# Three edits at the handover of a hashed-attention and feed-forward kernel: an earlier split, a later threshold, outputs added by transfer

## The chip, the cores and the metric

The kernel runs on one core of one Trainium2 chip. The metric is the device time of one execution in microseconds; the time before is the median of three runs, 980.2 us (979.35 to 982.82).

## What is computed

The first part is attention with a hash mask, for 4 batches of 8 heads, 768 rows and 64 columns a head; the second is a feed-forward network over the 3072 tokens of all batches, 512 to 2048 to 512.

```python
q_bits = (einsum('bhsd,dk->bhsk', q, proj) > 0)        # 6 bits a row; k likewise
mask = q_bucket[:, :, :, None] == k_bucket[:, :, None, :]
scores = np.where(mask, (1 / sqrt(64)) * q @ k.T, -1e9)
attn = softmax(scores)                                 # over the keys
x = (attn @ v).transpose(0, 2, 1, 3).reshape(3072, 512)
h = x @ w_in
g = h * np.clip(h + 3.0, 0.0, 6.0) / 6.0
out = g @ w_out
```

## The kernel before, in words

**Units of work.** There are 32 heads (i = 8 b + h) and 6 row tiles of 128 rows in each, so 192 row tiles, numbered g or k. Every fp32 operand is held as a rounded high part and a low part, and a product is the sum of two or three products of parts. The scores of a row tile are four matrix products on TensorE (lines 376 and 378); `lowest` (line 385, VectorE) takes the row minimum of the negated scores, `exponential` (397, ScalarE) the softmax numerator. P is then transposed, and `split_p` casts it into the high part ph (464, ScalarE) and subtracts for the low part pl (468, VectorE, or 466, GpSimd). Two row tiles make one output unit u (three in a head; unit numbers run from 0 to 95 over all heads): `values` or `values_whole` (489, 501) multiplies P by v into a bank acc of PSUM.

**Output of a unit.** `output` (lines 513 to 540) copies acc to the tile y (531, ScalarE). Half the rows of acc hold the product with v's high part, the other half that with its low part, and both have to be added. For most heads this is done in memory: one half is stored by a plain transfer from SyncE's queue (537) into xs, and the other half waits in the list `adds`, until `add` (508 to 511) sends it as an adding transfer from GpSimd's queue. For the last head of a batch (`last_head`, 526) ScalarE copies only one half (528), VectorE adds the other (529), and one plain store brings the sum.

**The order of the steps.** The engines' programs are in the order in which the Python code calls them for TensorE, VectorE, ScalarE and GpSimd, transfers issued from GpSimd among them; the order on SyncE's queue, from which all other transfers go, is left to the scheduler. The main loop runs over k. In step k it transposes tile k, takes the exponential of k + 1 and the minimum of k + 2, multiplies by v for an earlier unit, calls `lead(k + 3)` and splits tile k. `lead(j)`, with t = j mod 6, issues the scores of tile j and, depending on t, the preparation of the next heads: at t = 1 and 4 `add`, at t = 3 the hash products (`hash_qk`, 330 to 332) and their thresholding (`bits`, 341, VectorE, with a transfer of the result), at t = 4 `scale_q` (276, GpSimd).

Batch 0's feed-forward part runs as a block of its own, from 142 to 300 us. From k = 94 (`held`) the generator `ffn` is called in the loop and prepares the first chunk of 256 tokens of batch 1: it loads it (xr), inverts the softmax sums, spreads each inverse over 64 columns (`spread`, 559, GpSimd, one buffer), transposes that on TensorE (`rt`, 569, in one of the four banks that pt and acc also use) and multiplies (572, VectorE). Each piece is put beside a step: spread and rt pair of one quarter of the chunk follow each other through steps 95 to 99. From k = 101 (GT - 1) `beside_ffn` takes over: P is transposed by VectorE (`flip`, 418), written to memory (fd) and read back in the order wanted (`move`), and one sixteenth of a chunk's products goes beside each step (`gemm1`, 642; `gate`, 664, 665, 670, 671; `gemm2`, 680 to 685). The buffer p of a tile has two copies, so the minimum of tile 104 needs tile 102 to be written out. The first chunk's split into xh (631, ScalarE) and xl (632, VectorE) stands in the list `opening`, and line 1114 calls it in step 102, ahead of that step's first `gemm1`. A later chunk is begun when its units are out and no add of its batch is pending (`there`, 908).

Of the kernel before, what the change touches and what calls it, by code (L numbers as in the profile page):

```python
# [18 lines left out]
P = 128  # L19
# [9 lines left out]
LA = 3  # L29
# [14 lines left out]
def lsh_attention_moe(  # L44
# [11 lines left out]
    B, H, D, S = qkT.shape  # L56
    D //= 2
    DM, DF = w_in.shape
    KT = S // P
# [16 lines left out]
    def dma(out: bass.AP, in_: bass.AP):  # L76
        nonlocal last
        last = nc.sync.dma_start(out=out, in_=in_)  # L78
# [152 lines left out]
    GF = 2 * HK + FS  # L231
    GT = GF + FT
# [128 lines left out]
    scs, probs, outs = {}, {}, {}  # L361
# [53 lines left out]
    def flip(g: int):  # L415
        nonlocal written
        x = probs.pop(g)[0][:].rearrange("p c k -> p (c k)")
        nc.vector.transpose(x, x)  # L418
        d = dp.tile([P, S], F32, name=f"fd{g}", tag="fd", bufs=4)
        dma(out=d[:], in_=x)  # L420
        written[g] = d, last
# [84 lines left out]
    adds = []  # L506
# [6 lines left out]
    def output(un: int):  # L513
        nonlocal vdone
        i, u = divmod(un, KT // 2)
        b, h = divmod(i, H)
        o = (h % 2) * D
        acc = accs.pop(un)

        if u != 1:  # L520
            outs[i] = sp.tile([P, 4 * P if u == 0 else 2 * P], F32, name=f"y{i}_{u}", tag=f"y{u}", bufs=1)
        y = outs[i][:, 2 * P :] if u == 1 else outs[i][:, : 2 * P]

        r = slice(o, o + D)
        r2 = slice(D - o, 2 * D - o)
        last_head = h == H - 1 and (b > 0 or u == 2)
        if last_head:
            nc.scalar.copy(y[r], acc[r2])
            nc.vector.tensor_add(y[r], acc[r], y[r])
        else:  # L530
            nc.scalar.copy(y, acc[:])
        if u or last_head:
            c = slice(2 * u * P, 2 * (u + 1) * P) if last_head and b else slice(0, 4 * P) if u == 1 else slice(4 * P, S)
            to = xs[b][h * D : (h + 1) * D, c]

            with tc.issue_after(copied.ins):
                dma(out=to, in_=y[r] if last_head else outs[i][r])
            if not last_head:
                adds.append((i, to, outs[i][r2]))
        vdone = 2 * un + 2  # L540


# [33 lines left out]
    muls = []  # L576
# [132 lines left out]
    side, opening = [], []  # L709
# [366 lines left out]
    with tc.manual_schedule(engines={ET.PE, ET.DVE, ET.Activation, ET.Pool}):  # L1076
        split_qk(0, None)
        hash_qk(0)
        bits(0)
        scale_q(1)  # L1080
        split_v(0)
        for x in range(3):
            ahead(0, x)
        for _ in range(2):
            cv(0)
        def go(part: str):
            if stage == part:
                next(fill, None)

        through = []  # L1090

        def beside_ffn(k: int):

            nonlocal paced, stage, held
            held = False
            if k < GT:
                for c in range(2):
                    transp(k, c)  # L1100
                exponential(k + 1)
            for _ in range(2):
                u = vnext // 2
                if u < NS // 2 and (2 * u < GT or k % 2 and k >= 2 * u + 3):
                    if vnext % 2 == 0 and k >= GT:
                        value_whole()
                        through.append(u)
                        break
                    if value_half():
                        through.append(vnext // 2 - 1)  # L1110
                if k < GT:
                    break
            if k == GT:
                opening.pop()()
            if k + 2 < NS and k >= GT:
                lowest(k + 2)
            go("A")
            if k < GT:
                for c in range(2):
                    split_p(k, c, False)  # L1120
                split_lows()
                while through:
                    output(through.pop(0))
                flip(k + 1)
            if k + 2 < NS:
                if k < GT:
                    lowest(k + 2)
                exponential(k + 2)
            paced = True
            multiply()  # L1130
            if k + 2 < NS:
                flip(k + 2)
            if GT <= k - LT < NS:
                for c in range(2):
                    split_p(k - LT, c, False)
            split_lows()
            go("B")
            if k == NS + LT:
                homes.clear()
            while through and (through[0] < vnext // 2 - 1 or k % 2 == 0 or k < GT):  # L1140
                output(through.pop(0))
            hashed = k + LA < NS and (k + LA) % KT == 4 and (k + LA) // KT + 1 < NJ
            if hashed:
                hash_qk((k + LA) // KT + 1)
            go("C")
            if hashed:
                bits((k + LA) // KT + 1)
            if k + LA < NS:
                lead(k + LA)
            if moves:  # L1150
                moves.pop(0)()
            if GT <= k + 1 < NS:
                move(k + 1)

            place_in_chunk = (k - GT) % NFC
            if subs and (k % 2 and (k < GT or place_in_chunk != NFC - 1) or k > GT and place_in_chunk == 0):
                subs.pop(0)()
            go("D")
            if k % KT in (1, 3):
                add()  # L1160

        for k in range(NS + LT + 2):
            if k >= GT - 1:
                beside_ffn(k)
                continue
            end = GB if k < GB else NS
            i, t = divmod(k, KT)
            if k == HK - XE:
                lent += lents[cc3:]
            if k == GB:  # L1170
                lent.clear()
            if k == HK:
                late["x"] = sp.tile([P, S], F32, name="late", tag="raw", bufs=1)
            for c in range(2):
                transp(k, c)
            if k + 1 < end:
                exponential(k + 1)
            if k + 2 < end:
                lowest(k + 2)
            if k == GB:  # L1180
                next(first)
                pair_turn = 0

            third = True
            whole = False
            for _ in range(1 if k != HK else 2):
                if vnext < k - k % 2:
                    whole = value_half()
            held = k >= GF - 2
            if held:  # L1190
                next(fill, None)
            if whole and k >= GF:
                output(vnext // 2 - 1)
                whole = False

            hashed = k >= GF and (k + LA) % KT == 2
            if k >= GF and k + LA < end and not hashed:
                lead(k + LA)
            for c in range(2):
                split_p(k, c, third)  # L1200
            split_lows()
            multiply()
            held = False
            if (k < GF or hashed) and k + LA < end:
                if hashed:
                    if (k + LA) // KT + 1 < NJ:
                        hash_qk((k + LA) // KT + 1)
                        bits((k + LA) // KT + 1)
                    next(fill, None)
                lead(k + LA)  # L1210
            if k == GB - 2:
                hash_qk((GB - 1) // KT + 1)
                bits((GB - 1) // KT + 1)
            if whole:
                output(vnext // 2 - 1)
            if k >= GF - 2 and not hashed:
                next(fill, None)
            if k < GB:
                for f in early_steps[k]:
                    f()  # L1220

            if k < HK and t == 1 and i:
                with tc.issue_after(last.ins):
                    load_w(i)
            if k == HK:
                add()
                late_x()
                with tc.issue_after(last.ins):
                    get_qk(H + 2)
                    for n in range(WE, WL):  # L1230
                        load_w(n)
            if k + 1 == GB:
                first = first_ffn(lambda part: ahead(GB, part))
                next(first)
                for _ in range(2):
                    whole = value_half()
                output(vnext // 2 - 1)
                next(first)
        paced = False
        assert vnext == NS and not through  # L1240
        add()
        for _ in fill:
            pass
# [47 lines left out]
```

## Time and profile before

| what | value |
| --- | --- |
| median of three runs | 980.2 us |
| the profiled execution | 981.36 us |
| its span | 979.6 us |
| TensorE (PE) busy, granted clock | 953.1 us (97%), 0.998 |
| VectorE (DVE) busy | 715.7 us (73%) |
| ScalarE (ACT) busy | 626.7 us (64%) |
| GpSimd (POOL) busy | 479.2 us (49%) |
| adding transfers from GpSimd (line 510) | 57, 48.7 us |
| sums on VectorE (line 529) | 10, 4.3 us |
| chain that ended last: PE, DVE, issue | 77%, 9%, 4% |

Busy time is the time in which an engine executes; a row of the timeline gives start, duration, engine, line and operation, the number of instructions merged into it, and in brackets how long the engine was idle before and what ended that. A matrix product's row can overlap the next one, as products are pipelined. PEclk is the granted clock of TensorE as a share of 2.4 GHz.

### The profile page before, as it was taken

To read this page: it belongs to the slowest core of one execution; us is meant where nothing else is said; L and a number is where in the kernel's file an instruction comes from. 1 tells how busy PE (TensorE), PEld (TensorE's weight loads), DVE (VectorE), ACT (ScalarE), POOL (GpSimd) and SP (SyncE) were. 2 spreads that over 40 slices of the span, in tenths; PEclk is the share of its full clock that TensorE was granted. 3 is DMA by queue.
4 is the path that set the end of the run, shared out by engine and by line. 5 is a ranking of instruction groups with operands and counts; after the bars stand their busy time and mean duration, and the time that the engine had idled before them with its cause. 6 is when DMAs were issued, how large, how long until landed. Compare 5 with 4: busy or idle time off the path is not lost.

```text
span 979.6 us, 19386 instructions
## 1 busy us (share of the span) xinstructions
PE 953.1 (97%) x6306; PEld 874.4 (89%) x6306; DVE 715.7 (73%) x1462; ACT 626.7 (64%) x1421; POOL 479.2 (49%) x498
## 2 busy tenths in 40 slices
PE   8999999999999998899999999999999999999997
PEld 7999888999989998799889888998999899899896
DVE  7999988888569998777777777877777874343422
ACT  6898875656478897567766666766766664333332
POOL 6777744656537775355555545546556542000000
PEclk9999999999999999999999999999999999999999
DMA  4566579100035554687797787797797772101000
GB/s 118 138 165 174 132 229 376 46 2 1 6 121 130 117 114 118 184 246 235 217 274 231 230 244 234 225 272 231 233 267 228 220 222 78 43 1 44 1 22 22
DMA packets 113116, 151.65 MB, mean 155 GB/s; under 512 B 13764, under 2 KB 82116, under 8 KB 113016
## 3 DMA queue, kind: packets, MB, share of 16 engines
q1 hardware_dynamic: 108456, 144.79, 48.8%
q0 software_dynamic: 4560, 5.64, 4.6%
q8 instruction: 50, 0.82, 0.4%
q14 instruction: 50, 0.41, 0.1%
HBM read 77.34 MB, written 53.61 MB: 134 GB/s over the span
## 4 chain that ended last, share of the span: by engine, by line
PE 77%; DVE 9%; issue 4%; POOL 3%; DMA 3%; ACT 2%; SPq 1%; DVEq 0%; ACTq 0%; POOLq 0%
PE h L642 25%; PE po L685 6%; PE po L680 6%; PE po L681 6%; PE acc L489 6%; PE acc L501 5%; PE s L376 5%; PE pt L407 5%; PE s L378 5%; DVE p L385 3%; DVE pl L468 2%; POOL pl L466 2%; DVE qq L341 1%; DMA px<-fd 1%; SPq L78 1%
## 5 line engine op out<-in xcount | busy, mean ns | idle before, releaser
L397 ACT ACTIVATE p<-p,m 128x768 f32<-128x768 f32 x192 | 180.2, 938 | 97.0 <-DVE p L385 91.3
L385 DVE TENSOR_SCALAR_CACHE_REDUCE p<-s 128x768 f32<-128x768 f32 x192 | 183.0, 953 | 45.4 <-PE s L378 30.8
L665 DVE SCALAR_TENSOR_TENSOR h<-g,h 128x256 f32<-128x256 f32 x192 | 81.9, 427 | 95.2 <-ACT g L664 93.5
L664 ACT ACTIVATE g<-h,three 128x256 f32<-128x256 f32 x192 | 90.8, 473 | 91.4 <-PE h L642 89.7
L642 PE MATMUL h<-xh,w 128*128 128x256 f32 x1024 | 146.8, 283 | 1.6 <-ACT xh L631 1.6
L642 PEld LDWEIGHTS h<-xh,w 128*128 128x128 f32 x1024 | 135.5, 189 | 5.1 <-ACT xh L631 1.8
L418 DVE STREAM_TRANSPOSE p<-p 128x768 f32<-128x768 f32 x90 | 88.0, 978 | 60.3 <-ACT p L397 60.3
L466 POOL TENSOR_TENSOR pl<-spare,ph 128x384 fp32r<-128x384 f32 x45 | 62.1, 1381 | 119.0 <-ACT ph L464 82.8
L376 PE MATMUL s<-kk,qq 76*128 76x384 f32 x384 | 101.4, 345 | 4.8 <-DVE qq L341 3.0
L468 DVE TENSOR_TENSOR pl<-pt,ph 128x384 fp32r<-128x384 f32 x196 | 100.0, 550 | 3.6 <-ACT ph L464 3.0
L670 ACT CAST gb<-h 128x256 fp32r<-128x256 f32 x141 | 52.4, 372 | 76.1 <-DVE h L665 43.1
L378 PE MATMUL s<-kk,qq 128*128 128x384 f32 x384 | 100.6, 343 | 0.0
L681 PE MATMUL po<-w,gb 128*128 128x512 f32 x250 | 98.4, 394 | 0.0
L680 PE MATMUL po<-w,gb 128*128 128x512 f32 x250 | 98.4, 394 | 0.0
L466 POOL TENSOR_TENSOR pl<-px,ph 128x384 fp32r<-128x384 f32 x45 | 61.3, 1362 | 75.2 <-ACT ph L464 66.0
L464 ACT CAST ph<-pt 128x384 fp32r<-128x384 f32 x196 | 85.9, 472 | 15.1 <-PE pt L407 13.1
L216 POOL TENSOR_TENSOR w<-wr,w 128x128 fp32r<-128x128 f32 x128 | 71.8, 591 | 45.3 <-ACT w L210 42.4
L407 PE MATMUL pt<-ident,p 128*128 128x128 f32 x612 | 86.0, 274 | 3.6 <-DVE pl L468 2.7
L407 PEld LDWEIGHTS pt<-ident,p 128*128 128x128 f32 x612 | 71.7, 141 | 11.2 <-PE pt L407 2.5
L376 PEld LDWEIGHTS s<-kk,qq 76*128 76x128 f32 x384 | 65.7, 190 | 17.9 <-DVE qq L341 8.0
L642 PE MATMUL h<-xl,w 128*128 128x256 f32 x512 | 81.5, 281 | 0.0
L685 PE MATMUL po<-w,gb 128*128 128x512 f32 x250 | 78.7, 395 | 0.0
(153 smaller groups left out, 2130.9 us busy)
## 6 DMA issues: line engine op xcount, KB each, us to landing
fd<-p SPq DMA_DIRECT2D x90, 384.0 KB, 3.0
spare<-fd SPq DMA_DIRECT2D x180, 96.0 KB, 2.6
px<-fd SPq DMA_DIRECT2D x180, 96.0 KB, 3.2
kk<-qq SPq DMA_DIRECT2D x62, 192.0 KB, 3.3
wr<-in_w_in SPq DMA_DIRECT2D x16, 512.0 KB
wr<-in_w_out SPq DMA_DIRECT2D x16, 512.0 KB, 7.5
raw<-in_qkT SPq DMA_DIRECT2D x19, 384.0 KB, 3.8
vr<-in_v SPq DMA_DIRECT2D x32, 192.0 KB, 3.4
```

The costliest lines, as they stand in the source:

```text
L376: nc.tensor.matmul(s[:, c, :HW], lhsT=q1[:KM, us], rhs=half(k1[:KM], c), start=True, stop=False)
L378: nc.tensor.matmul(s[:, c, :HW], lhsT=q2[:, us], rhs=half(k2, c), start=False, stop=True)
L385: nc.vector.tensor_scalar(out=pr_[:], in0=s[:, :, :HW], scalar1=CAP, scalar2=None, op0=ALU.min, op1=ALU.min, accum_out=m[:],)
L397: nc.scalar.activation(pr_[:], pr_[:], AF.Exp, bias=m[:], scale=-1.0, accum_out=sms[b][:, t, h : h + 1])
L407: nc.tensor.transpose(pt[:, x], probs[g][0][:, c, x * P : (x + 1) * P], ident[:])
L466: engine.tensor_sub(lo, pt, hi.bitcast(F32))
L468: lows.append(lambda: engine.tensor_sub(lo, pt, hi.bitcast(F32)))
L642: nc.tensor.matmul(hp, lhsT=wi[:, wp, wc], rhs=x[cc][xp], start=(k == 0 and cc == 0), stop=(k == 2 and cc == NCC - 1),)
L664: nc.scalar.activation(r[:], hp, AF.Relu, bias=three[:], scale=1.0)
L680: nc.tensor.matmul(po[u], lhsT=gh[:, us], rhs=wo[:, 0], start=(fc == 0), stop=False)
L681: nc.tensor.matmul(po[u], lhsT=gh[:, us], rhs=wo[:, 1], start=False, stop=False)
L685: nc.tensor.matmul(po[u], lhsT=gl[:, us], rhs=wo[:, 0], start=False, stop=(fc == NFC - 1))
```

## The change

It does three things. In `output`, for batches 1 to 3, only the first unit (u = 0) of the last head is still added on VectorE; the second and the third are copied in full, one half is stored and the other goes into `adds`. The call of `opening` moves from the beginning of step 102 to step 101, behind `flip(102)` and ahead of `lowest(103)` and `exponential(103)`. In the plain loop from k = 96 on, a step with (k + 3) mod 6 = 3 calls `lead` behind `split_p`, `split_lows` and `multiply`, as one with remainder 2 already did; in that step `lead` holds the hash products, the scores and `bits`.

```diff
-        last_head = h == H - 1 and (b > 0 or u == 2)
+        last_head = h == H - 1 and u == (0 if b else 2)
...
         if u or last_head:
-            c = slice(2 * u * P, 2 * (u + 1) * P) if last_head and b else slice(0, 4 * P) if u == 1 else slice(4 * P, S)
+            alone = last_head or h == H - 1 and b
+            c = slice(2 * u * P, 2 * (u + 1) * P) if alone else slice(0, 4 * P) if u == 1 else slice(4 * P, S)
             to = xs[b][h * D : (h + 1) * D, c]
 
             with tc.issue_after(copied.ins):
-                dma(out=to, in_=y[r] if last_head else outs[i][r])
+                dma(out=to, in_=y[r] if alone else outs[i][r])
             if not last_head:
-                adds.append((i, to, outs[i][r2]))
+                adds.append((i, to, y[r2] if alone else outs[i][r2]))
...
-            if k == GT:
-                opening.pop()()
             if k + 2 < NS and k >= GT:
                 lowest(k + 2)
             go("A")
...
                 flip(k + 1)
+                assert len(side) <= 2 and not muls
+                opening.pop()()
             if k + 2 < NS:
                 if k < GT:
                     lowest(k + 2)
...
             hashed = k >= GF and (k + LA) % KT == 2
-            if k >= GF and k + LA < end and not hashed:
+            after = hashed or k >= GF and (k + LA) % KT == 3
+            if k >= GF and k + LA < end and not after:
                 lead(k + LA)
...
-            if (k < GF or hashed) and k + LA < end:
+            if (k < GF or after) and k + LA < end:
```

## Rows read from the trace of the kernel before

**Rows 1.** Stretches: length, busy time (instructions) of each engine, PEclk, DMA share, GB/s
```profile
380.00:400.00 20.00, 17.40 (x125) 15.59 (x123) 16.12 (x33) 12.27 (x28) 8.75 (x9) 1.00 0.36 101
400.00:410.00 10.00, 7.35 (x38) 6.59 (x37) 6.42 (x15) 5.61 (x15) 0.00 (x0) 0.83 0.80 241
```

**Rows 2.** PE's waits, 380 to 412: total us, times, longest us
```profile
PE h L642 <- ACT xh L631: 1.6, 1, 1.6
PE pt L407 <- DVE pl L468: 1.5, 3, 1.0
PE rt L569 <- DVE y L529: 1.1, 1, 1.1
```

**Rows 3.** Timeline, VectorE and ScalarE, steps 96 to 102
```profile
381.97 0.48 ACT L464 CAST ph<-pt 128x384 fp32r<-128x384 f32 x1 [0.46 <-PE acc L489]
...
383.43 1.09 DVE L341 TENSOR_SCALAR qq<-z,thr,val 44x768 fp32r<-44x768 f32 x1 [0.86 <-issue]
...
384.55 1.02 DVE L468 TENSOR_TENSOR pl<-pt,ph 128x384 fp32r<-128x384 f32 x2
...
386.99 0.37 ACT L528 COPY y<-acc 64x256 f32<-64x256 f32 x1 [3.35 <-PE acc L489]
...
388.14 0.43 DVE L529 TENSOR_TENSOR y<-acc,y 64x256 f32<-64x256 f32 x1
...
401.54 0.98 DVE L418 STREAM_TRANSPOSE p<-p 128x768 f32<-128x768 f32 x1 [1.15 <-ACT p L397]
402.44 1.39 DVE L632 TENSOR_TENSOR xl<-xr,xh 128x256 fp32r<-128x256 f32 x4
```

**Rows 4.** Timeline, TensorE, steps 96 to 102
```profile
383.89 0.39 PE L569 MATMUL rt<-ident,spare 128*128 128x128 f32 x2
385.26 0.98 PE L407 MATMUL pt<-ident,p 128*128 128x128 f32 x6 [0.98 <-DVE pl L468]
...
388.72 0.41 PE L569 MATMUL rt<-ident,spare 128*128 128x128 f32 x2 [1.05 <-DVE y L529]
...
391.21 0.38 PE L569 MATMUL rt<-ident,spare 128*128 128x128 f32 x2
...
394.61 0.52 PE L407 MATMUL pt<-ident,p 128*128 128x128 f32 x3 [0.24 <-DVE pl L468]
...
401.85 2.36 PE L642 MATMUL h<-xh,w 128*128 128x256 f32 x8 [1.60 <-ACT xh L631]
```

**Rows 5.** Groups of instructions: busy us, mean ns, idle before, releaser
```profile
L531 ACT COPY y<-acc 128x256 f32<-128x256 f32 x86 | 31.6, 368 | 6.8 <-PE acc L489 4.8
```

**Rows 6.** Timeline, SyncE's queue and GpSimd, steps 88 to 98
```profile
365.86 0.46 SPq L78 DMA_DIRECT2D xs<-y  x1
...
368.63 0.83 POOL L510 DMA_DIRECT2D xs<-y  x1 [1.57 <-DMA xs<-y]
...
387.98 2.14 POOL L276 TENSOR_SCALAR raw<-raw 64x768 f32<-64x768 f32 x1 [3.18 <-DMA raw<-in_qkT]
390.07 0.39 POOL L559 COPY spare<-rc 128x256 f32<-128x256 f32 x1
```

**Rows 7.** PE's waits, 412 to 820
```profile
PE acc L501 <- POOL pl L466: 1.8, 8, 0.3
```

**Rows 8.** Timeline, GpSimd, first chunk of the last batch
```profile
829.83 0.40 POOL L559 COPY spare<-rc 128x256 f32<-128x256 f32 x1 [2.71 <-PE rt L569]
```

**Rows 9.** Stretches of one microsecond behind the first product, columns as in rows 1
```profile
403.00:404.00 1.00, 1.00 (x5) 1.00 (x6) 0.83 (x3) 0.00 (x0) 0.00 (x0) 0.50 1.06 424
```

**Rows 10.** The chain that ended last, 398 to 413: start us, us, what
```profile
400.75 3.49 DMA fd<-p
404.35 0.98 DVE p L385 x2
...
407.71 0.88 DVE p L385 x2
...
412.66 0.62 PE s L376 x2
```

## The prediction

> **What bounds the kernel now.** I read the page's busy shares first: TensorE (PE) is busy for 97% of the span, the others for 73% at most. So an edit that moves work of other engines pays only where PE stands still. The table of stretches shows where: from 380 to 400 us PE misses 2.6 of 20, and from 400 to 410, where attention hands over to the mixed phase, 2.65 of 10, at a mean granted clock of 0.83 [rows 1]. The three edits act in steps 95 to 102, some 376 to 410 us, and one of them also at the last heads of batches 2 and 3. Next come PE's waits from 380 to 412: 1.6 us for the first token chunk's rounded halves (xh), 1.5 in three for P's low parts, the longest 1.0, and 1.1 for the output add on VectorE (DVE) [rows 2]. These are what the three edits touch. The profiled run took 981.36 us, 1.76 of them outside its span of 979.6; the median of the runs is 980.2, 1.16 lower. I work out differences in the profiled run and put them on the median. About 0.5%, 4.9 us, is what a measurement of this kernel can tell from no change.
>
> **Bits behind the low parts.** The condition holds once in the plain loop: for k from 96 to 100, (k+3) mod 6 is 3 only at k = 96, and the case that was there before, 2, does not come. In that step DVE sits idle for 0.86 us, then runs head 17's bits at 383.43 for 1.09, then both low parts in 1.02; the ph casts that these need end at 382.45 (381.97 + 0.48) [rows 3]. PE has finished the rt transposes at 384.28 and waits until 385.26, 0.98 us, because the next pt tiles take the banks that the low parts free [rows 4]. Swapped, the low parts start at about 382.6 and the banks are free at 383.6, before PE asks. The bits start at 383.6 instead of 383.43, and their transfer goes out 0.2 later; head 17's scores are three steps off, which hides that. The PE order does not change, since the step issues nothing for PE between the two places. The gain is 0.98 here. It could be 0 if DVE's next wait swallowed it, but the value products and the y copy that follow wait for PE alone.
>
> **Last heads' units.** Each of three batches loses two adds on DVE (0.43 each) and gets two adding transfers from GpSimd (POOL). The ScalarE copies stay, 128 rows wide instead of 64: 368 ns on average [rows 5] against the 0.37 us of the one at 386.99 [rows 3], so no cost. What goes: rt at 388.72 waits 1.05 us for the add of unit 47, done at 388.57; with the copy alone the bank is free at 387.36, when the copy ends. Less the 0.98 from above, both waits are gone, and PE would come to the third rt pair at 391.21 - 0.98 - 1.05 = 389.2 [rows 3, 4].
>
> What comes is a wait. Units 46 and 47 are put out in steps 95 and 97, and the next call of add() is in step 97, inside lead(100), right behind the output of unit 47. Its transfer can't start before that unit's plain store has landed. The rows show the same wait at the head before: store issued at 365.86, add at 368.63 after 1.57 us of idle POOL, that is 2.77 from store to add, then 0.83 for the add [rows 6]. Behind the adds in POOL's order stand scale_q(18), 2.14 us, and then the spread that feeds the third rt pair; they began at 387.98 and 390.07, and the spread was done 0.75 before PE took it at 391.21 [rows 4, 6]. Now: y copy at 386.99 - 0.98 = 386.0, done 386.4; store issued then, landed 389.2; add until 390.0; scale_q until 392.1; spread until 392.5. PE reaches the pair at 389.2 and stands until 392.5: the pair is 1.3 us **later** than before, though two waits are gone. PE's wait of 0.24 at 394.61, behind it, is then covered [rows 4], so I take 1.0 later at the end of the stretch. Bounds: a gain of 2.0, if the adds hold nothing up, and a loss of 1.3 without any recovery. I take the loss, because rows 6 show the same instruction behind the same store. Unit 46's add is free: its store is two steps old, and POOL is idle at that time.
>
> In batches 2 and 3 the adds go out a step behind the store, as at all other heads, and cost POOL 4 x 0.83 us in all. POOL's low parts hold up PE eight times for 1.8 us, 0.3 at most, from 412 to 820 [rows 7], so the bound is 4 x 0.3 = 1.2; I take 0, since the adds of other heads stand in the same places. The very last add, after the loop, stands ahead of a spread of the last batch, before which POOL idles 2.71 us [rows 8], enough for 0.83 and most of a store's landing. It takes 0.
>
> **First token's splits.** The four casts (ScalarE) and four subtractions (DVE, 1.39 in all) move from behind the exponential of row tile 103 to ahead of its row minimum [rows 3]. PE's 1.6 of waiting goes [rows 2], and so may the stretch at 0.50 of the clock that follows it. In the 10 us to 410 a mean of 0.83 makes 3.4 us at 0.50 (1.2 GHz), which is 1.7 us of PE work [rows 1, 9]. The full gain would be 3.3. I take 0, because the chain that ends last does not pass there. It goes from the transposed P of tile 102 through its transfer (issued 400.75, 3.49 us) to the row minimum of 104 at 404.35, which reuses that buffer, on through the exponential and the transpose of 104 to the minimum of 105 at 407.71 and head 18's bits, and only then do the scores of 106 run on PE at 412.66 [rows 10]. PE work that comes earlier now stands still before the hash of head 18, which needs the minimum of 105. On the cost side the splits delay minimum, exponential and transpose of 103 by 1.39: the transpose ends at 403.9 instead of 402.5 (401.54 + 0.98) [rows 3] and, at the same 3.49, its transfer lands at 407.4, still ahead of 407.71. If SyncE's order pushed it further back, up to 1.4 would be lost.
>
> On the clock: after PE's idle stretch of 1.60 up to 401.85 the granted clock was 0.50 from 403 to 404 [rows 4, 9]; here that was hidden under the chain. The Trainium skill, TensorE: Matmul & The Clock Gate, section "HAM oscillation — how this bites in real kernels", says that a PE left waiting for data falls back to the low clock and pays for it in the next burst, so work should be kept contiguous. By that rule, with which this row agrees, the new stand from 389.2 to 392.5 would be paid for too, and the sum would be 982.9; that is the second rival below.
>
> **Sum:** bits -0.98, DVE add -1.05, POOL's hold-up +3.3 (389.2 to 392.5), recovered -0.24, splits 0: +1.0. 980.2 + 1.0 = **981.2 us**.
>
> **Rivals.** (1) The adds hold nothing up: a faster store or another place of it on SyncE's queue lets the spread come in time. For it: the queue's order is not written by hand. Against: the 2.77 us of rows 6. Then -2.0: 978.2. (2) **Slower**: the stand before the third rt pair lets the clock fall, in a stretch where PE is the bound and nothing hides it. It decides once PE stands clearly longer than the 1.60 us ahead of 401.85. Price: the same 3.4 us at half, 1.7, on top of the 1.0: 982.9. Against: the waits of 0.98 and 1.05 are shorter and left no such mark in the mean clock of 380 to 400, 1.00 [rows 1]. (3) The first product was the bound after all, and the adds hold nothing up: 0.98 + 1.05 + 1.6 + 1.7 = 5.3, so 974.9. For it: these are the largest waits on PE. Against: the chain of rows 10. (4) The change does nothing: a wait beside each takes its place: 980.2.
>
> **How the numbers follow.** Forecast 0.42, rival 1 0.22, rival 2 0.16, rival 3 0.13, rival 4 0.07. Only rival 3 is faster by over 0.5% (below 975.3): 0.13. Slower by over 0.5% (above 985.1) needs rival 2 with the 1.4 of the late transfer and the 1.2 of POOL on top, 0.04 of its 0.16. Same: 0.83. The range leaves out rival 3 and that corner: below, rival 1 with half of the splits' 3.3, 976.5; above, rival 2 with part of the late transfer, 984.0.
>
> **What would show it.** Right: in step 97 two adds on POOL, the second waiting for its store; PE's waits for the low parts in step 96 and for DVE's y add gone; a new wait before the third rt pair of about 3 us; no wait for xh, but a longer one before head 18's hash, and the scores of 106 about 1 us later than 412.66. Wrong: no wait before the third rt pair (rival 1), granted clock at 0.50 between 392 and 397 (rival 2), or the scores of 106 before 409 (rival 3). If SyncE's order changes in the mixed phase and PE's waits there move by several us, the whole sum misses its place.

## The result and the profile after

The changed kernel is slower by a little: ratio 1.0022 to the kernel before, interval 1.0012 to 1.0032, which is 2.2 us. The medians of the 20 runs of each are 983.06 and 980.62 us, 2.4 apart. The profiled execution took 981.87 us, its span 980.1. The forecast was 981.2 against 980.2, 1.0 us slower: the right direction and inside the stated range, but a little below the measured interval of 1.2 to 3.2 us.

The order on SyncE's queue differs from before only around the handover, from 397 to 411 us, and from 416 to 820 no wait of PE is longer than 0.3 us (before, 0.5), so the traces are compared from 370 to 416. PE's waits there (total us, times, longest us), against [rows 2]:

```profile
PE z L330 <- DVE p L385: 3.8, 1, 3.8
PE rt L570 <- POOL spare L560: 2.6, 1, 2.6
PE pt L407 <- DVE pl L468: 1.2, 2, 0.9
PE s L376 <- DVE p L385: 0.5, 1, 0.5
```

The waits for xh and for the y add are gone. Two longer ones stand in their place: 2.6 us before the third rt pair, and 3.8 before head 18's hash (z). The second is hardly new idle time: before, PE stood 1.6 us for xh, 1.05 before that hash and 1.26 before the scores of 106, 3.9 in all. The timeline of PE shows where, against [rows 4, 10]:

```profile
379.37 0.51 PE L376 MATMUL s<-kk,qq 76*128 76x384 f32 x2
...
383.20 0.38 PE L570 MATMUL rt<-ident,spare 128*128 128x128 f32 x2
383.42 0.82 PE L407 MATMUL pt<-ident,p 128*128 128x128 f32 x6
...
385.50 0.41 PE L570 MATMUL rt<-ident,spare 128*128 128x128 f32 x2
...
387.11 0.52 PE L407 MATMUL pt<-ident,p 128*128 128x128 f32 x3 [0.87 <-DVE pl L468]
...
391.83 0.44 PE L570 MATMUL rt<-ident,spare 128*128 128x128 f32 x2 [2.61 <-POOL spare L560]
...
399.47 0.52 PE L376 MATMUL s<-kk,qq 76*128 76x384 f32 x2
...
410.17 0.62 PE L330 MATMUL z<-qq,pjl 128*108 128x384 f32 x1 [3.83 <-DVE p L385]
...
414.10 0.63 PE L376 MATMUL s<-kk,qq 76*128 76x384 f32 x2
```

PE came to the third rt pair at 391.83 - 2.61 = 389.22 and stood until 391.83. The scores of 106 start at 414.10 instead of 412.66. The timelines show the reason, against [rows 6]. ScalarE has the y copy:

```profile
384.99 0.37 ACT L531 COPY y<-acc 128x256 f32<-128x256 f32 x1 [2.03 <-PE acc L489]
```

SyncE issues unit 47's store behind it:

```profile
385.42 0.47 SPq L78 DMA_DIRECT2D xs<-y  x1
```

GpSimd's queue:

```profile
384.24 0.83 POOL L510 DMA_DIRECT2D xs<-y  x1
388.42 0.80 POOL L510 DMA_DIRECT2D xs<-y  x1 [3.35 <-ACT ph L464]
389.00 2.42 POOL L276 TENSOR_SCALAR raw<-raw 64x768 f32<-64x768 f32 x1
391.09 0.68 POOL L560 COPY spare<-rc 128x256 f32<-128x256 f32 x1
```

The second add stands on POOL's queue for 3.35 us, which the profile puts down to a cast; the cast writes nothing that the add reads, and the add starts 3.00 us after its store was issued. What it waits for is the landing of that store: the last update of the store's semaphore, for which the add waits, is in the trace at 387.88, and the add starts 0.54 later. At the head before [rows 6] these are 368.08 and 0.55, in the run a_alone below 389.20 and 0.55. Behind the add come scale_q and the spread. Stretches of one microsecond show the clock (the columns are those of [rows 1]):

```profile
391.00:392.00 1.00, 0.17 (x2) 0.18 (x3) 0.00 (x0) 0.00 (x0) 0.77 (x2) 1.00 0.00 0
...
393.00:394.00 1.00, 1.00 (x6) 1.00 (x6) 0.93 (x2) 0.00 (x0) 0.91 (x2) 0.50 0.00 0
394.00:395.00 1.00, 1.00 (x5) 1.00 (x5) 0.00 (x0) 0.75 (x3) 1.00 (x1) 0.50 0.27 65
395.00:396.00 1.00, 1.00 (x6) 0.90 (x5) 0.97 (x3) 1.00 (x2) 0.93 (x2) 0.50 0.99 264
...
410.00:411.00 1.00, 0.83 (x3) 0.82 (x4) 0.35 (x3) 0.90 (x2) 0.00 (x0) 0.50 1.05 344
411.00:412.00 1.00, 1.00 (x5) 0.93 (x4) 0.84 (x1) 1.00 (x5) 0.00 (x0) 0.50 0.83 254
```

After the first stand, and from the end of the second on, the granted clock is 0.50, 1.2 GHz. Before, the only such stretch between 376 and 420 was that of [rows 9], from 402.8 to 406.

Profiled executions reach the handover up to 2.9 us apart, so the runs are compared by lengths: S1 from the start of tile 98's scores on PE to that of 104's, and S2 from there to 106's. Tile 98's start at 379.52 us before and 379.37 after, 104's at 397.95 and 399.47, 106's at 412.66 and 414.10. The timeline of PE before:

```profile
379.52 0.52 PE L376 MATMUL s<-kk,qq 76*128 76x384 f32 x2
...
397.95 0.52 PE L376 MATMUL s<-kk,qq 76*128 76x384 f32 x2
...
408.72 0.40 PE L330 MATMUL z<-qq,pjl 128*108 128x384 f32 x1 [1.05 <-DVE p L385]
```

The runs are told one by one below.

| run | S1, us | S2, us | S1 + S2, against before | ratio of times (95%) |
| --- | --- | --- | --- | --- |
| before | 18.43 | 14.71 | | 1 |
| changed kernel | 20.10 | 14.63 | +1.6 | 1.0022 (1.0012 to 1.0032) |
| b_alone | 19.58 | 14.41 | +0.9 | 1.0011 (1.0001 to 1.0020) |
| c_alone | 17.72 | 15.36 | -0.1 | 1.0011 (1.0003 to 1.0020) |
| a_alone | 20.86 | 14.20 | +1.9 | 1.0036 (1.0023 to 1.0049) |
| adds_later | 18.46 | 15.40 | +0.7 | 1.0014 (1.0003 to 1.0024) |
| adds_split | 16.06 | 15.29 | -1.8 | 0.9983 (0.9974 to 0.9993) |
| adds_split_late_first | 16.76 | 14.10 | -2.3 | 0.9982 (0.9973 to 0.9991) |
| fill_wait | 19.20 | 14.76 | +0.8 | 1.0013 (1.0004 to 1.0022) |
| later_batches_only | 18.15 | 14.25 | -0.7 | 0.9990 (0.9981 to 0.9999) |

The intervals of the times are about 1 us to either side, and lengths of one execution differ by some tenths: later_batches_only has the same handover as the kernel before, and comes out 0.7 us shorter there. Differences below that in a whole length are not argued from; pieces behind one wait scatter less, as the run fill_wait shows.

### The profile page after: what moved, and what is told of

The parts are those of the page before. It is cut to its first block, busy times and chain, and to the rows that moved or that the text cites. A ratio compares the mean times of both kernels' runs of the same rounds, so it can differ in the third digit from the quotient of the medians.

```text
span 980.1 us, 19383 instructions
## 1 busy us (share of the span) xinstructions
PE 953.2 (97%) x6306; PEld 875.3 (89%) x6306; DVE 712.7 (73%) x1456; ACT 626.4 (64%) x1421; POOL 486.2 (50%) x504
## 4 chain that ended last, share of the span: by engine, by line
PE 78%; DVE 8%; POOL 3%; issue 3%; ACT 2%; DMA 2%; SPq 1%; DVEq 0%; ACTq 0%; POOLq 0%
PE h L643 25%; PE po L681 6%; PE po L686 6%; PE po L682 6%; PE acc L489 6%; PE acc L501 5%; PE s L376 5%; PE s L378 5%; PE pt L407 5%; DVE p L385 3%; DVE pl L468 2%; POOL pl L466 2%; SPq L78 1%; ACT ph L464 1%; DVE qq L341 1%
```

## The experiments

The theory (theory A in the expectations) was that the adds in step 97 are what costs, since they stand on POOL ahead of the spread. Its rivals were that the earlier splits cost (rival C), and that the three edits act independently (theory S).

### The bits behind the low parts, alone

Run b_alone:

```diff
+            after = hashed or k >= GF and (k + LA) % KT == 3
-            if k >= GF and k + LA < end and not hashed:
+            if k >= GF and k + LA < end and not after:
                 lead(k + LA)
...
-            if (k < GF or hashed) and k + LA < end:
+            if (k < GF or after) and k + LA < end:
```

> The kernel before with the bits behind P's low parts and nothing else. If the adds ahead of the spread are what costs (theory A): no loss here; and hardly a gain, because VectorE still stands for the load of the chunk until 386.8 and the add of unit 47 comes behind that, so the wait of 0.98 us for the low parts goes and the wait for the y add grows by as much: 0 to -0.5 us, scores of 106 between 412.2 and 412.7. If the three edits are independent (theory S, the sum of part 2 of the prediction): -0.98 us, scores of 106 at 411.7.

Measured: 1.0011, 1.1 us longer, and S1 is longer by 1.15; neither expectation had that. PE's waits from 370 to 416 have the wait for the y add doubled:

```profile
PE rt L569 <- DVE y L529: 2.1, 1, 2.1
```

The stretches of the same run:

```profile
389.00:390.00 1.00, 1.00 (x9) 0.87 (x9) 1.00 (x3) 0.74 (x3) 1.00 (x1) 0.92 0.08 22
390.00:391.00 1.00, 1.00 (x5) 1.00 (x6) 1.00 (x4) 0.25 (x2) 0.83 (x2) 0.50 0.18 44
...
392.00:393.00 1.00, 1.00 (x6) 0.90 (x5) 0.14 (x1) 0.27 (x2) 0.00 (x0) 0.50 0.00 0
```

The wait moved, as theory A has it: 0.98 and 1.05 became one of 2.12. That the clock falls after the joined one was in neither expectation, and it makes the edit alone a loss: up to the second rt pair S1 is 0.27 us shorter than before (8.93 against 9.20), and from there to the scores of 104, where the low stretch lies, 1.4 longer (10.65 against 9.23).

### The first token's splits, alone

Run c_alone:

```diff
-            if k == GT:
-                opening.pop()()
...
                 flip(k + 1)
+                assert len(side) <= 2 and not muls
+                opening.pop()()
```

> The kernel before with the first token's splits a step ahead and nothing else. Theory A: PE's wait for xh goes and a wait before head 18's hash takes its place, because the chain through the transfer of tile 102 ends last: 0 us, at most +0.5. Rival C (the earlier splits are what costs, by their 1.4 us on VectorE ahead of the minimum of 103): +1 to +2.4 us, scores of 106 at 413.7 or later.

Measured: 1.0011, 1.1 us longer (0.3 to 2.0); S2 is 0.65 longer. PE's timeline has no wait for xh, and a long one before the hash:

```profile
407.17 0.63 PE L330 MATMUL z<-qq,pjl 128*108 128x384 f32 x1 [3.90 <-DVE p L385]
...
411.75 0.65 PE L376 MATMUL s<-kk,qq 76*128 76x384 f32 x2
```

The stretches of the same run, behind that wait:

```profile
408.00:409.00 1.00, 1.00 (x5) 0.93 (x4) 0.84 (x1) 1.00 (x5) 0.00 (x0) 0.50 0.91 254
```

No gain, as the chain of [rows 10] said, but the time alone does not decide between the two: 1.1 us is above the 0.5 of theory A and at the lower end of rival C, and the interval reaches into both. Against the trace of the kernel before, the whole 0.65 lies behind the hash, from there to the scores of 106, where the clock is low (4.58 against 3.94 us). Up to the hash S2 is as long as before (10.78 against 10.77); but the other four runs with the splits at their old place need only 10.17 to 10.35 there, so that some 0.5 of VectorE's delay, rival C's way, may be hidden by a slow execution of the kernel before. S1 is shorter by 0.7 in this execution, though the edit does not reach into it; that is the scatter.

### The adds by transfer, alone

Run a_alone. The diff is the part of the change in `output`.

> The kernel before with the adds by transfer and nothing else. Theory A: the y copy stays at 387, so store, add, scale_q(18) and spread end at about 390, 391, 393 and 393.4, and the third rt pair stands at 393.4 instead of 391.2; with the low clock behind it +2 to +3 us. Rival C: no loss, and the wait for the y add gone, -1 us.

Measured: 1.0036, 3.5 us, the largest loss of all. GpSimd's timeline:

```profile
389.75 0.80 POOL L510 DMA_DIRECT2D xs<-y  x1 [4.10 <-ACT ph L464]
390.33 2.42 POOL L276 TENSOR_SCALAR raw<-raw 64x768 f32<-64x768 f32 x1
392.42 0.68 POOL L560 COPY spare<-rc 128x256 f32<-128x256 f32 x1
```

The rt pair stands until 393.15, within 0.3 us of the expected 393.4. So the adds cost by themselves. In the traces the bits' edit gives back a part of it in the changed kernel (S1 of 20.10 against 20.86); the intervals of the two times overlap. The rival that the adds cost nothing falls, and so does theory S: alone the three edits come to 1.1, 1.1 and 3.5 us, 5.7 together, against the 2.2 of the change.

### The adds moved behind the spread, both

Run adds_later:

```diff
-        if t in (1, 4) and not paced:
+        if t in (1, 4) and not paced and j != GF + 4:
             add()
...
+            if k == GF + 2:
+                add()
```

> The changed kernel, but the adds of units 46 and 47 are issued at the end of step 98, behind the spread of the third quarter, instead of in step 97. Theory A: the spread is there when PE comes to the third rt pair at 389.2, no wait and no low clock before 397; against the changed kernel -3 to -3.5 us, against the kernel before -1.5 to -2.0, so a ratio of 0.998 to 0.9985. Rival C: as the changed kernel, 1.002.

Measured: 1.0014, no gain against the kernel before; theory A's 0.998 to 0.9985 was missed, and by the time alone rival C would stand. The third rt pair no longer waits, and S1 falls by 1.6 to 18.46. But the fourth pair waits 1.71:

```profile
395.70 0.41 PE L570 MATMUL rt<-ident,spare 128*128 128x128 f32 x2 [1.71 <-ACT y L531]
```

The copy of unit 48 writes the tile y0, of which there is one buffer, and unit 46's late add still reads it. That is the code's dependence; that the fourth pair's wait comes from it the next run shows, which moves unit 46's add back and nothing else.

### Only unit 47's add moved

Run adds_split:

```diff
-    def add():
-        for _, to, of in adds:
+    def add(n=None):
+        for _, to, of in adds[:n]:
             nc.gpsimd.dma_start(out=to, in_=of, accum_op=ALU.add)
-        adds.clear()
+        del adds[:n]
...
-            add()
+            add(1 if j == GF + 4 else None)
...
+            if k == GF + 2:
+                add()
```

> The changed kernel, but in step 97 only unit 46's add is issued and unit 47's waits until the end of step 98, behind the spread. So neither the spread nor the y copy of unit 48 (which stood behind unit 46's late add in the run with both adds moved) is held up. Theory A: from the scores of tile 98 to those of tile 104 some 16.8 us (18.43 before, 20.10 in the changed kernel), no low clock there; behind it the earlier splits keep the chain at 15 us, so -1 us against the kernel before, -2.7 against the changed one: ratio 0.999. Rival C (the splits cost, not the adds): 20 us and 1.002.

Measured: 0.9983, faster than the kernel before by 1.7 us and than the changed one by 3.8 (1.0022 against 0.9983). On GpSimd's timeline the spread ends at 389.85, ahead of the third rt pair:

```profile
385.77 0.83 POOL L510 DMA_DIRECT2D xs<-y  x1
387.36 2.14 POOL L276 TENSOR_SCALAR raw<-raw 64x768 f32<-64x768 f32 x1 [0.76 <-DMA raw<-in_qkT]
389.45 0.40 POOL L560 COPY spare<-rc 128x256 f32<-128x256 f32 x1
390.77 0.40 POOL L560 COPY spare<-rc 128x256 f32<-128x256 f32 x1 [0.92 <-PE rt L570]
391.29 0.89 POOL L510 DMA_DIRECT2D xs<-y  x1
```

PE's timeline of the same run has that pair without a wait:

```profile
390.25 0.38 PE L570 MATMUL rt<-ident,spare 128*128 128x128 f32 x2
```

S1 is 16.06 against 18.43 before and 20.10 in the changed kernel. The early splits are in this run too, so rival C, by which it would have come out at 1.002, falls. One add, 0.83 us of GpSimd's time and its place behind a store, decides between a gain and a loss.

### The same, with the splits at their old place

Run adds_split_late_first: the diff of the run before, without the move of `opening`.

> As the run adds_split, with the first token's splits at their old place in step 102. Theory A with the chain as told in the prediction (the splits are worth 0): the same as adds_split. If they cost, by VectorE's 1.4 us ahead of the minimum of 103: from the scores of 104 to those of 106 14.3 instead of 15.0 to 15.4 us, and 0.5 to 1 us faster than adds_split: ratio 0.998. If they gain: slower than adds_split by up to 3.3.

Measured: 0.9982. In time it is the same as with the early splits. In the trace S2 is 1.2 us shorter, 14.10 against 15.29. VectorE's timeline of this run:

```profile
398.81 0.08 DVE L385 DVE_READ_ACCUMULATOR p<-s 128x1 f32 x1
400.05 0.98 DVE L418 STREAM_TRANSPOSE p<-p 128x768 f32<-128x768 f32 x1 [1.16 <-ACT p L397]
400.95 1.39 DVE L633 TENSOR_TENSOR xl<-xr,xh 128x256 fp32r<-128x256 f32 x4
402.26 0.95 DVE L385 TENSOR_SCALAR_CACHE_REDUCE p<-s 128x768 f32<-128x768 f32 x1
```

The same in adds_split, with the early splits:

```profile
398.99 1.43 DVE L633 TENSOR_TENSOR xl<-xr,xh 128x256 fp32r<-128x256 f32 x4 [0.48 <-ACT xh L632]
400.34 0.95 DVE L385 TENSOR_SCALAR_CACHE_REDUCE p<-s 128x768 f32<-128x768 f32 x1
401.22 0.08 DVE L385 DVE_READ_ACCUMULATOR p<-s 128x1 f32 x1
402.40 0.98 DVE L418 STREAM_TRANSPOSE p<-p 128x768 f32<-128x768 f32 x1 [1.10 <-ACT p L397]
403.30 0.92 DVE L385 TENSOR_SCALAR_CACHE_REDUCE p<-s 128x768 f32<-128x768 f32 x1
```

At the old place the subtractions run while VectorE would wait for the transfer of tile 102 (in the kernel before it stood another 0.52 us for it behind them); early, they run ahead of minimum, exponential and transpose of 103 and delay them, and the minimum of 104 follows that transpose directly. Of the 1.2 us 0.53 lie ahead of the hash and 0.66 behind it, where the clock is low with the early splits and full without them. Whether the 1.2 us reach the end stays open: S1, which the move does not reach, is 0.7 longer in this trace, and the times differ by 0.1 us, each with an interval of about 1 us.

### PE kept at work through the wait

Run fill_wait:

```diff
     rt = bank([P, TC], f"rt{name}", tag)
+    if name == "1_0_2":
+        for _ in range(22):
+            nc.tensor.transpose(rt[:, :P], ident[:], ident[:])
```

> The changed kernel with 22 transposes of the identity in front of the third rt pair, into the pair's own bank and overwritten by it: PE works through its wait for the spread instead of standing, and nothing else moves. Prices the low clock by itself: if the clock is what the wait costs on top (rival 2 of the prediction), the granted clock stays at 1.00 from 392 to 397 and the scores of 104 come 1.2 to 1.7 us earlier than in the changed kernel (18.4 to 18.9 us behind those of 98, against 20.10); if the low clock was hidden, 20.1.

Measured: 1.0013, against 1.0022 of the changed kernel; the intervals overlap. On PE's timeline the wait is filled:

```profile
388.77 2.56 PE L571 MATMUL rt<-ident 128*128 128x128 f32 x22
...
391.93 0.44 PE L573 MATMUL rt<-ident,spare 128*128 128x128 f32 x2 [0.60 <-POOL spare L560]
```

The stretch behind it keeps its clock:

```profile
393.00:394.00 1.00, 1.00 (x10) 1.00 (x9) 0.94 (x2) 0.22 (x1) 0.91 (x2) 1.00 0.00 0
```

S1 is 19.20 against 20.10: the low clock costs 0.9 us here, less than the 1.2 to 1.7 expected, and the wait itself the other 0.8 against the 18.43 before. One execution's lengths scatter by 0.7, but the piece behind the wait does not: from the third rt pair to the scores of 104 it is 6.67 to 6.74 us in the six runs where the clock is full and PE meets no wait but one of 0.24, this one among them (6.68), and 7.64 in both runs with the low stretch there, the changed kernel and a_alone. The wait of 0.24 us for low parts that the kernel before has at 394.61 [rows 4] is there in this run too, though the pair is as late as in the changed kernel:

```profile
395.27 0.52 PE L407 MATMUL pt<-ident,p 128*128 128x128 f32 x3 [0.24 <-DVE pl L468]
```

In the changed kernel it is gone.

### Adds by transfer at batches 2 and 3 alone

Run later_batches_only:

```diff
-        last_head = h == H - 1 and (b > 0 or u == 2)
+        last_head = h == H - 1 and (u == (0 if b else 2) or b == 1)
```

The rest of `output` is as in the change.

> The kernel before with the adds by transfer for the last heads of batches 2 and 3 alone; batch 1 adds on VectorE as before. Theory A (the cost sits in step 97, with batch 1): 0, ratio between 0.999 and 1.001. If the adds cost at every last head, by POOL's 0.83 us each ahead of the low parts: up to +1.2 us.

Measured: 0.9990 (0.9981 to 0.9999), as expected no loss. The cost sits with batch 1.

## Why the prediction was right, and where it was off

The direction and the first half of the mechanism held. The changed kernel is slower because unit 47's add holds up GpSimd ahead of the spread; a_alone shows the adds' cost alone, adds_split takes it away. The other half was the second rival's: a granted clock at 0.50 between 392 and 397 was its sign, it came, and its 2.7 us lies in the measured 1.2 to 3.2, the forecast's 1.0 just below. That the forecast came as near as it did is partly luck, since a hold-up taken 0.7 us too long stood against a clock priced at nothing, which cost 0.9. Step by step:

- **Bits.** The wait of 0.98 us at 385.26 [rows 4] is gone, though as a term of its own the 0.98 was wrong: alone the edit only moves the wait to the y add (b_alone, 2.12). With the adds off VectorE the sum of both terms held: PE came to the third rt pair at 389.22; 389.2 was predicted. That it fits so closely is luck: a new wait of 0.87 (next point) stands against a wait of 0.32 at 381.05, which is gone too, and a start 0.15 earlier.
- **DVE add.** Gone, as said. Not in the sum: unit 46's plain store no longer waits for VectorE either, so the chunk's load behind it on SyncE's queue was issued 1.4 us earlier (380.65 against 382.07), and VectorE's stand for it ended earlier (385.20 against 386.81). A wait of 0.87 for low parts came in one step later.
- **POOL's hold-up.** Predicted to last until 392.5, measured 391.83: the y copy ran 1.0 earlier than taken, store to add took 3.00 instead of 2.77, scale_q 2.42 instead of 2.14. The spread took 0.68 instead of 0.39. The 3.3 of the sum was 2.6.
- **The recovered 0.24.** The sum took PE's wait at 394.61 as covered because the pair comes later. In fill_wait the pair is as late and the wait stands; only at the low clock is it gone. So without the low clock nothing was recovered; the 0.9 that the low clock cost has these 0.24 already taken off.
- **The clock.** This is the step that failed, a term left at nothing: "I take 1.0 later at the end of the stretch", with the low clock only in the second rival. It came, at 0.50 from 393 to 396, and cost 0.9 of the 1.67 us by which S1 grew (fill_wait). The rival's 1.7 was too much, as a part of a low stretch overlaps work that waits for other engines anyway. Of that the wait of 0.24 is shown; for the rest the explanation is only argued.
- **The splits at 0.** PE's wait for xh was worth nothing, as the chain said: c_alone is not faster. But that the chain goes through the transfer of tile 102 to the minimum of 104 did not hold: with the splits early this minimum follows VectorE's transpose of 103 directly. And the long stand before the hash brought a low clock that [rows 10] had no place for. S2 grows by 0.65 in c_alone and by 1.2 between the two adds_split runs, and the times give 1.1 (0.3 to 2.0) and 0.1 us. So the splits cost between nothing and some 1 us, and which it is stays open.
- **Batches 2 and 3** at 0: later_batches_only, 0.9990.

## What to carry to other kernels

A plain store and an adding transfer onto the same bytes make one serial piece: from store to add 2.5 us in a_alone and 3.0 in the changed kernel, and then 0.8 for the add. Here scale_q and the spread, behind the add on GpSimd's queue, waited for all of it; put the add where nothing urgent stands behind it, and look which buffer it keeps. Waits of one engine that stand one behind another are no independent terms: taking the first away handed its time to the second (b_alone), and the one long stand cost more than the two short ones, because of the clock. A wait on the busiest engine is worth nothing while the chain that ends last passes by it: c_alone took away 1.6 us of waiting and gained nothing.

## What the runs showed that was not expected

- Two waits of PE, 0.98 and 1.05 us with work between them, left the granted clock at 1.00; joined to one of 2.12 (b_alone) it was followed by a stretch at 0.50, and so were 2.61 and 3.83 (changed kernel).
- The length of a stand alone does not tell whether the clock falls. The stand of 1.60 us before the first product was followed by 0.50 in the kernel before [rows 4, 9] and in later_batches_only, but not in adds_split_late_first (1.60), b_alone (1.61) and a_alone (1.70); nor were 1.71 in adds_later and 1.73 in adds_split_late_first. Between 370 and 416 us of the ten traces every stand from 1.91 us up was followed by it. What else decides stays open. From adds_split_late_first:

```profile
400.37 1.78 PE L643 MATMUL h<-xh,w 128*128 128x256 f32 x8 [1.60 <-ACT xh L632]
```

```profile
401.00:402.00 1.00, 1.00 (x8) 0.88 (x8) 1.00 (x5) 0.23 (x1) 0.00 (x0) 1.00 0.48 141
```

- A stretch at low clock of about 3.5 us, filled with products and transposes, cost 0.9 us of length in the changed kernel and 1.4 in b_alone, less than half of itself.
- An add that is issued too late costs as well: unit 46's, moved by a step and a half, held up a copy into the tile it reads from, and PE for 1.71 us.
